# Two transformer layers on one core: the first two chains of each second MLP product issued together, and the first MLP rows normalised earlier

## Chip, core and metric

The kernel runs on one core of a Trainium2 chip. The metric is the device time of one execution in microseconds (us). TensorE (PE) multiplies; its sums lie in PSUM, 8 banks of 128 x 512 fp32. VectorE (DVE), ScalarE (ACT) and GpSimd (POOL) do the rest; SyncE (SP) issues nearly all DMAs. The engines run side by side, each works through its own list in order, and semaphores tie them together.

## The reference

An attention block and an MLP, both with a layer norm ahead and a residual, are applied twice with the same weights. 2048 rows of width 640, 32 heads of 20, hidden width 1536:

```python
x = x + _A_ref(_layernorm(x), wqkv, wo)            # softmax attention
x = x + _B_ref(_layernorm(x), w1, b1, w2, b2)
x = x + _A_ref(_layernorm(x), wqkv, wo)
x = x + _B_ref(_layernorm(x), w1, b1, w2, b2)

def _B_ref(x, w1, b1, w2, b2):
    h = einsum("bsd,df->bsf", x, w1) + b1
    r = where(h > 0, h, 0)
    return einsum("bsf,fd->bsd", r * r, w2) + b2
```

## The kernel before

Matrix operands are kept as two parts, hi (rounded) and lo (the rest), and a product is three matmuls: hi x hi, hi x lo, lo x hi (`THREE`, L323). A **chain** (L333) is the run of matmuls that sum into one PSUM bank; its first sets `start`, its last `stop`. `ps_all` (L95) hands out the 8 banks in turn, one for each chain, so a bank comes round again eight chains later.

`layer` (L1333) does one layer: the QKV projection, attention, and then, with all rows in four blocks of 512 (`qb`, each of four tiles `i` of 128 rows):

- **Output projection**, `add_heads` (L1240). For each of 4 row tiles and 2 halves of the width (`hf`), a chain of 15 matmuls (128x320), then a DVE add of the sum onto the row tile x (L1255), then `side()`. After both halves the tile is stored to `x_mid` in DRAM.
- **Transposing**, `transposed` (L1272), for the first MLP block only: the four normalised row tiles are turned by 20 PE transposes (L1277: five 128-column pieces k, four tiles i each), and each piece is split by ACT (hi, L256) and DVE (lo, L257) into `xnT`.
- **MLP**, `mlp` (L1285), four blocks, each in two halves of the hidden width (`fh`). The first product: for six tiles f of hidden units a chain of 15 matmuls (128x512); then ACT adds the bias and clips (r, L1300), DVE squares (L1301), ACT rounds to the hi part of h (L256), DVE forms its lo part (L257). The second product: for `hf` in 2 and `i` in 4 a chain of 18 matmuls (128x320), called y0 to y7 below, over the six h tiles in the order in which they were made, three matmuls each. So the last three matmuls of a chain read the newest h tile: two its hi part, one its lo part. A DVE add (L1320) takes the sum onto the row tile, then `side()`. In the first half POOL adds the bias b2 to the row tiles (L1307) after their loads; after y0 of the second half the next block's `xnT` is split from rows that were turned through DRAM (`parts`, L292, on ACT, DVE and POOL).

`side()` takes the next entry of a list `steps` and runs it: this is how work for what comes next gets between the chains. Ahead of the last output-projection block, `steps` gets ten entries that step the generator `normal_rows` (L1259) once each: the first issues the loads of rows 0 to 511 from `x_mid` on SP (L1261), four take the statistics of a tile (DVE L244 twice and L245, then two small POOL operations L247 and L248), four normalise a tile on DVE (L252), and the tenth ends it. The block has 8 chains, called C1 to C8 below, so eight entries run there; `all_steps()` behind it runs the other two. The order of each engine's work is that of the code; nothing reorders it.

After the projection SP has, in this order, the last of the `x_mid` stores, the loads of the rest of w1 and all of w2 (19 tiles of 480 to 512 KB), and the loads of the row tiles for the MLP.

## Time and profile before

| | us |
|---|---|
| median of 3 runs (lowest, highest) | 3569.83 (3569.45, 3570.3) |
| the profiled execution: its own time | 3570.51 |
| its span, first to last instruction | 3568.7 |

| stage, first layer | from about, us | to about, us |
|---|---|---|
| output projection, last block (C1 begins before the first add at 1434.96) | 1433 | 1450.0 |
| transposes of the first MLP rows | 1450.0 | 1453.8 |
| first MLP block, first product of the first half | 1453.8 | 1474.3 |
| its second product, y0 to y7 | 1474.3 | 1496.1 |
| second half: first product, second product | 1496.1 | 1538.3 |
| three more blocks | 1538.3 | 1797.6 |

The MLP of the second layer runs from 3226.8 to the end of the span. In the profile, an instruction's row gives the start, the duration, the engine, the line, output and inputs, how often it is merged, and in brackets how long its engine sat idle before it and who released it. Matmuls are pipelined: a 128x320 matmul is recorded with about 310 ns, while 127 of them in a row start at 1477.34 and the next ones at 1496.07, which is one each 147.5 ns.

### The profile page before, as it was taken

How to read it: one execution, taken by the hardware profiler on the slowest of the kernel's cores; microseconds unless marked ns; L12 is line 12 of the kernel's file. 1: busy time of each engine (PE TensorE's matmuls, PEld its weight loads, DVE VectorE, ACT ScalarE, POOL GpSimd, SP SyncE). 2: the span in 40 equal slices, each digit the busy share in tenths (PEclk: the TensorE clock that was granted, in tenths of full speed). 3: DMA queues.
4: the chain of work that ended last, by engine and by line, in shares of the span. 5: the costliest groups of instructions: out<-in, count | busy, mean ns of one | idle time of the engine just before them, and what ended most of it. 6: DMA issues, size and time to landing. Idle time of an engine off the chain costs nothing.

```text
span 3568.7 us, 70878 instructions
## 1 busy us (share of the span) xinstructions
PE 3551.0 (100%) x25544; PEld 2147.5 (60%) x25544; DVE 2636.6 (74%) x5088; ACT 2701.5 (76%) x4720; POOL 817.0 (23%) x929
## 2 busy tenths in 40 slices
PE   9999999999999999999999999999999999999999
PEld 7898333333333336889989973333333333378998
DVE  7998888888888881455569988888888888625443
ACT  5888999999999994122248889999999999932221
POOL 4430334321211210122153201212121212101110
PEclk9999999999999999999999999999999999999999
DMA  7666454422212136622367652232222121375221
GB/s 254 224 210 187 143 166 144 145 79 79 54 48 61 53 103 224 230 74 74 104 199 226 199 164 72 74 78 58 70 82 57 45 56 51 112 240 204 78 80 36
DMA packets 281598, 431.87 MB, mean 121 GB/s; under 512 B 70948, under 2 KB 130084, under 8 KB 281248
## 3 DMA queue, kind: packets, MB, share of 16 engines
q1 hardware_dynamic: 280720, 425.64, 38.6%
q8 instruction: 203, 3.33, 0.4%
q10 hardware_dynamic: 528, 1.70, 0.2%
q14 instruction: 147, 1.20, 0.1%
HBM read 282.52 MB, written 144.68 MB: 120 GB/s over the span
## 4 chain that ended last, share of the span: by engine, by line
PE 96%; ACT 1%; DMA 1%; DVE 1%; issue 0%; POOL 0%; SPq 0%; ACTq 0%; DVEq 0%; POOLq 0%
PE banks L771 28%; PE banks L336 22%; PE banks L756 18%; PE banks L662 17%; PE banks L356 6%; PE banks L368 5%; ACT e L766 1%; PE banks L351 1%; PE banks L469 0%; DMA kd<-d_kd 0%; DVE h L257 0%; DVE r L1301 0%; ACT r L1300 0%; ACT h L256 0%; SPq L76 0%
## 5 line engine op out<-in xcount | busy, mean ns | idle before, releaser
L766 ACT ACTIVATE e<-banks 128x512 f32<-128x512 f32 (+1 forms) x3416 | 2037.3, 690 | 49.3 <-PE banks L756 10.7
L673 DVE TENSOR_REDUCE mx<-banks 128x1 f32<-128x512 f32 x2560 | 1620.7, 685 | 322.6 <-PE banks L662 270.7
L771 PE MATMUL banks<-e,vg 128*32 128x512 f32 x8192 | 1093.4, 605 | 2.3 <-ACT e L766 2.3
L662 PE MATMUL banks<-k,q 60*128 60x512 f32 x3360 | 1060.4, 410 | 0.0
L756 PE MATMUL banks<-q,k 62*128 62x512 f32 x4096 | 1047.9, 441 | 0.7
L756 PEld LDWEIGHTS banks<-q,k 62*128 62x128 f32 x4096 | 515.4, 184 | 748.3 <-ACT e L766 493.5
L662 PEld LDWEIGHTS banks<-k,q 60*128 60x128 f32 x3360 | 566.3, 185 | 196.6 <-ACT e L766 65.6
L702 DVE CUSTOM_DVE_ANT_0 rl<-banks,rl 128x512 f32<-128x512 f32 x736 | 477.0, 689 | 36.2 <-PE banks L662 12.4
L695 ACT ACTIVATE rl<-banks 128x512 f32<-128x512 f32 x736 | 399.0, 601 | 58.1 <-PE banks L662 47.3
L771 PEld LDWEIGHTS banks<-e,vg 128*32 128x32 f32 x8192 | 162.2, 108 | 353.5 <-issue 271.1
L336 PE MATMUL banks<-w,h 128*128 128x320 f32 x2304 | 348.9, 310 | 2.7 <-DVE h L257 2.5
L1300 ACT ACTIVATE r<-banks,b_t 128x512 f32<-128x512 f32 x96 | 66.2, 689 | 375.6 <-PE banks L336 249.2
L336 PEld LDWEIGHTS banks<-w,h 128*128 128x128 f32 x2304 | 339.2, 188 | 11.4 <-DVE h L257 6.4
L336 PE MATMUL banks<-xnT,w 128*128 128x512 f32 x1440 | 329.7, 389 | 0.0
L368 PE MATMUL banks<-xnT,wqk 64*128 64x512 f32 x1080 | 326.5, 392 | 0.0
L356 PE MATMUL banks<-xnT,wqk 64*128 64x512 f32 x1080 | 326.2, 394 | 0.0
L336 PEld LDWEIGHTS banks<-xnT,w 128*128 128x128 f32 x1440 | 269.6, 188 | 55.3
L815 POOL TENSOR_TENSOR few<-few,minus_t 128x16 f32<-128x16 f32 x62 | 179.8, 2900 | 241.1 <-DMA few<-d_s 240.9
L662 PE MATMUL banks<-kd,q 60*128 60x512 f32 x736 | 211.3, 398 | 3.0 <-ACT rl L695 2.4
L368 PEld LDWEIGHTS banks<-xnT,wqk 64*128 64x128 f32 x1080 | 201.2, 187 | 9.2
L356 PEld LDWEIGHTS banks<-xnT,wqk 64*128 64x128 f32 x1080 | 199.0, 186 | 10.9 <-issue 1.7
L826 POOL TENSOR_TENSOR o<-o 128x512 f32<-128x512 f32 x62 | 79.5, 1283 | 519.1 <-DMA o<-d_r 280.5
(93 smaller groups left out, 2648.4 us busy)
## 6 DMA issues: line engine op xcount, KB each, us to landing
q<-d_qk SPq DMA_DIRECT2D x876, 80.0 KB
d_qk<-ev SPq DMA_DIRECT2D x80, 512.0 KB
k<-d_qk SPq DMA_DIRECT2D x444, 80.0 KB
x<-d_x SPq DMA_DIRECT2D x96, 320.0 KB
d_o<-ot SPq DMA_DIRECT2D x248, 80.0 KB
ot<-d_o SPq DMA_DIRECT2D x38, 512.0 KB
d_v<-v SPq DMA_DIRECT2D x32, 512.0 KB
vg<-d_v SPq DMA_DIRECT2D x32, 512.0 KB
```

The costliest lines, as they stand in the source:

```text
L336: nc.tensor.matmul(dst, a, b, start=(n == 0), stop=(n == last))
L356: top = nc.tensor.matmul(dst, a[:64], b[:64], start=start, stop=last)
L368: low = nc.tensor.matmul(dst, a, b, start=False, stop=last, skip_group_check=True)
L662: nc.tensor.matmul(dst, q_t[t][b : b + 60, p, sub * P : (sub + 1) * P], k_t[t // NQB, c][b : b + 60, p, :], start=True, stop=True,)
L673: nc.vector.tensor_reduce(maxima(t)[:, 2 * p + par, sub, c : c + 1], dst, axis=AX.X, op=ALU.max)
L695: nc.scalar.activation(r, dst, AF.Relu)
L702: nc.vector.tensor_tensor_reduce(out=r[par], in0=dst, in1=r[par], scale=1.0, scalar=LEAST, op0=ALU.add, op1=ALU.max, accum_out=maxima(t)[: ...
L756: nc.tensor.matmul(dst, k_t[t // NQB, kt // 4][b : b + 62, p, (kt % 4) * P : (kt % 4 + 1) * P], q_t[t][b : b + 62, p, :], start=True, stop ...
L766: nc.scalar.activation(dst, src, AF.Exp, scale=SCALE)
L771: nc.tensor.matmul(acc[32 * h : 32 * h + 32, :], v_t[t // NQB, kt // 8][:, kt % 8, 32 * h : 32 * h + 32], es[p][:, par, :], start=(kt == 0 ...
L815: nc.gpsimd.tensor_tensor(few, few, minus_t, op=ALU.pow)
L826: nc.gpsimd.tensor_mul(o[:, 0, :], o[:, 0, :], o[:, 1, :])
```

## The change

```diff
-    def chain(dst, pairs):
+    def chain(dst, pairs, part=None):
         last = len(pairs) - 1
-        for n, (a, b) in enumerate(pairs):
+        for n, (a, b) in list(enumerate(pairs))[part or slice(None)]:
             nc.tensor.matmul(dst, a, b, start=(n == 0), stop=(n == last))
...
             for hf in range(2):
                 c = slice(hf * HALF, (hf + 1) * HALF)
-                for i in range(4):
-                    dst = ps_all("y")
-                    chain(dst[:, :HALF], [
+                dsts = [ps_all("y") for _ in range(2)]
+
+                def down(i, part=None):
+                    chain(dsts[i][:, :HALF], [
                         (hs[f % 6][:, hx, i * P : (i + 1) * P], w_2.piece(at_2(f, hw, hf)))
                         for f in range(fh * 6, fh * 6 + 6)
                         for hx, hw in THREE
-                    ])
-                    x = xs[i]
+                    ], part)
+
+                for i in range(4):
+                    if i > 1:
+                        dsts.append(ps_all("y"))
+                    if hf or i > 1:
+                        down(i)
+                    elif i == 0:
+                        for part in (slice(15), slice(15, 18)):
+                            for j in range(2):
+                                down(j, part)
+                    x, dst = xs[i], dsts[i]
                     nc.vector.tensor_add(x[:, c], dst[:, :HALF], x[:, c])
...
                 norm = normal_rows(0, x_m, rows)
-                steps.extend([lambda: next(norm, None)] * 10)
+                steps.extend([lambda: (next(norm, None), next(norm, None))] * 5)
             add_heads(qb, x_a, x_m, xs, side)
```

Of each second product (16 in all: 2 layers, 4 blocks, 2 halves) the chains y0 and y1 are now issued as four pieces: 15 matmuls of y0, 15 of y1, the last 3 of y0, the last 3 of y1. Matmuls, banks and their turn are as before. The generator that loads and normalises the first MLP rows is stepped twice behind each of C1 to C5, in place of once behind each of C1 to C8 and twice behind the block.

PE in the first MLP block, second product: h_16523 is the fifth h tile, h_16547 the newest, w_... are tiles of w2; the rows stand at the end of y0 and at the end of y1.

```order
@@ -6226,5 +6226,4 @@
 L336 MATMUL banks<-w_16386,h_16523 128x320
 L336 MATMUL banks<-w_16384,h_16523 128x320
-L336 MATMUL banks<-w_16386,h_16547 128x320 x3
 L336 MATMUL banks<-w_16380,h_16430 128x320 x3
 L336 MATMUL banks<-w_16380,h_16451 128x320
@@ -6236,5 +6235,5 @@
 L336 MATMUL banks<-w_16386,h_16523 128x320
 L336 MATMUL banks<-w_16384,h_16523 128x320
-L336 MATMUL banks<-w_16386,h_16547 128x320 x3
+L336 MATMUL banks<-w_16386,h_16547 128x320 x6
 L336 MATMUL banks<-w_16380,h_16430 128x320 x3
 L336 MATMUL banks<-w_16380,h_16451 128x320
```

The newest tile is first read as the 16th matmul of the product before, as the 31st now, behind the 15 of y1.

DVE in the last block of the first layer's output projection: x_16019 is the block's first row tile, x_16054 its second, x_16183 to x_16189 are the four MLP row tiles. First the place where their statistics begin, before:

```order
L1255 TENSOR_TENSOR x_16019<-banks,x_16019 128x320 x2
L244 BN_STATS bst_16207<-x_16183 128x6 x2
L245 BN_AGGR mv_16208<-bst_16207 128x2
L1255 TENSOR_TENSOR x_16054<-banks,x_16054 128x320
L244 BN_STATS bst_16231<-x_16185 128x6 x2
L245 BN_AGGR mv_16232<-bst_16231 128x2
```

and now:

```order
L1255 TENSOR_TENSOR x_16019<-banks,x_16019 128x320
L244 BN_STATS bst_16191<-x_16183 128x6 x2
L245 BN_AGGR mv_16192<-bst_16191 128x2
L1255 TENSOR_TENSOR x_16019<-banks,x_16019 128x320
L244 BN_STATS bst_16214<-x_16185 128x6 x2
L245 BN_AGGR mv_16215<-bst_16214 128x2
L244 BN_STATS bst_16221<-x_16187 128x6 x2
L245 BN_AGGR mv_16222<-bst_16221 128x2
L1255 TENSOR_TENSOR x_16054<-banks,x_16054 128x320
```

The first statistics stand ahead of the add of C2 instead of behind it. Then, on the same engine, the end of the block (x_16089 and x_16124 are its last two row tiles, the last row is the first split for the MLP), before:

```order
L1255 TENSOR_TENSOR x_16089<-banks,x_16089 128x320
L252 TENSOR_SCALAR x_16183<-x_16183,mv_16208 128x640
L1255 TENSOR_TENSOR x_16124<-banks,x_16124 128x320
L252 TENSOR_SCALAR x_16185<-x_16185,mv_16232 128x640
L1255 TENSOR_TENSOR x_16124<-banks,x_16124 128x320
L252 TENSOR_SCALAR x_16187<-x_16187,mv_16255 128x640
L252 TENSOR_SCALAR x_16189<-x_16189,mv_16279 128x640
L257 TENSOR_TENSOR xnT_16349<-banks,xnT_16349 128x512
```

and now:

```order
L252 TENSOR_SCALAR x_16183<-x_16183,mv_16192 128x640
L1255 TENSOR_TENSOR x_16054<-banks,x_16054 128x320
L252 TENSOR_SCALAR x_16185<-x_16185,mv_16215 128x640
L252 TENSOR_SCALAR x_16187<-x_16187,mv_16222 128x640
L1255 TENSOR_TENSOR x_16089<-banks,x_16089 128x320
L252 TENSOR_SCALAR x_16189<-x_16189,mv_16246 128x640
L1255 TENSOR_TENSOR x_16089<-banks,x_16089 128x320
L1255 TENSOR_TENSOR x_16124<-banks,x_16124 128x320 x2
L257 TENSOR_TENSOR xnT_16349<-banks,xnT_16349 128x512
```

The last two normalisations stood behind the add of C8; now the last one stands behind the add of C5 and ahead of those of C6 to C8. On SP, ACT and POOL the order of the instructions is the same before and after.

## The prediction

> **What bounds the kernel now.** The page says first that PE is busy throughout, at the full granted clock in all 40 slices:

> ```profile
> span 3568.7 us, 70878 instructions
> PE 3551.0 (100%) x25544; PEld 2147.5 (60%) x25544; DVE 2636.6 (74%) x5088; ACT 2701.5 (76%) x4720; POOL 817.0 (23%) x929
> PEclk9999999999999999999999999999999999999999
> ```

> The change removes no matmul, so it can give back only time in which PE stands still or starts late. I therefore read next the list of PE's own waits:

> ```profile
> PE banks L336 <- DVE h L257: 2.5, 15, 0.2
> PE banks L1277 <- DVE x L252: 2.2, 4, 0.9
> ```

> These are the two waits that the two edits aim at: matmuls of the second product that wait for the lo part of the newest h, in 15 of 16 products, and transposes that wait for a normalised row. Together 4.7 us of idle time. But idle time is measured from the recorded end of the matmul before, and a recorded matmul (0.31 us) is more than twice as long as the distance at which matmuls follow one another. So I count by starts, in the timeline of PE around one block:

> ```profile
> 1474.30 2.88 PE L336 MATMUL banks<-w,h 128*128 128x320 f32 x17
> 1477.34 18.89 PE L336 MATMUL banks<-w,h 128*128 128x320 f32 x127 [0.17 <-DVE h L257]
> 1496.07 20.59 PE L336 MATMUL banks<-xnT,w 128*128 128x512 f32 x90
> 1516.50 2.94 PE L336 MATMUL banks<-w,h 128*128 128x320 f32 x17
> 1519.61 18.89 PE L336 MATMUL banks<-w,h 128*128 128x320 f32 x127 [0.17 <-DVE h L257]
> ```

> From 1477.34 to 1496.07 there are 127 matmuls, one each (1496.07 - 1477.34) / 127 = 0.1475 us. The 17 ahead of the wait should take 17 x 0.1475 = 2.51 us. They take 1477.34 - 1474.30 = 3.04 us in the first half and 1519.61 - 1516.50 = 3.11 us in the second. **So PE loses 0.53 us and 0.60 us there**, not 0.17. The second layer shows the same (3.05 and 3.10 us in its first and last half):

> ```profile
> 3247.32 2.88 PE L336 MATMUL banks<-w,h 128*128 128x320 f32 x17
> 3250.37 0.85 PE L336 MATMUL banks<-w,h 128*128 128x320 f32 x4 [0.17 <-DVE h L257]
> ...
> 3542.91 2.94 PE L336 MATMUL banks<-w,h 128*128 128x320 f32 x17
> 3546.01 0.56 PE L336 MATMUL banks<-w,h 128*128 128x320 f32 x2 [0.17 <-DVE h L257]
> ```

> [...]

> **First edit: the order of y0 and y1.** The timeline at the end of y0 shows when the parts of the newest h are there:

> ```profile
> 1475.94 0.62 ACT L256 CAST h<-r 128x512 fp32r<-128x512 f32 x1 [0.76 <-DVE r L1301]
> 1476.60 0.69 DVE L257 TENSOR_TENSOR h<-r,h 128x512 fp32r<-128x512 f32 x1 [0.69 <-ACT h L256]
> 1476.61 0.30 PEld L336 LDWEIGHTS banks<-w,h 128*128 128x128 f32 x2 [0.23 <-ACT h L256]
> ```

> The hi part is there at 1476.56 (PE's weight load waited for it), the lo part at 1477.29, by work of ACT and DVE that the edit doesn't touch. Now 30 matmuls stand ahead of the newest tile: hi is needed at 1474.30 + 30 x 0.1475 = 1478.73 and lo, the 33rd matmul, at 1474.30 + 32 x 0.1475 = 1479.02. The margins are 2.2 and 1.7 us, so the wait goes whole. In the second half everything is 0.07 us later; the margin stays over 1.6 us. Gain: 8 first halves x 0.53 + 7 second halves x 0.60 = 4.24 + 4.20 = **8.4 us**. (The sixteenth product, in the first layer's last block, has transposes of the next layer between the last first-product chain and y0, and had no wait.)

> What is late next? y0 ends at its 33rd matmul rather than its 18th: its add comes 1479.02 - 1477.34 = 1.7 us later than before, y1's add 0.4 us earlier (36th matmul at 1474.30 + 35 x 0.1475 = 1479.46, against 1477.34 + 18 x 0.1475 = 1480.0). Behind y0's add DVE has side work and, in the second half, eight small subtractions for the next block. No row after it is needed by PE soon: the bank comes round only after eight chains, and in the first block the adds already run far behind without PE waiting, because they wait for POOL's bias add:

> ```profile
> 1480.76 0.49 DVE L1320 TENSOR_TENSOR x<-banks,x 128x320 f32<-128x320 f32 x1 [3.47 <-POOL x L1307]
> ```

> y0's bank is first wanted again by the chain that begins at 1496.07, now 2 us earlier, 13 us behind that add. This cover, seven chains of 2.65 us, would have to be gone before the edit cost anything. Cost taken: 0.

> One thing has no row: PE returning to a sum that it left open in another bank. Each pair has 3 changes of bank where it had 1, so 32 more in all. A plain change of bank shows nothing: the 127 matmuls hold seven, at 0.1475 us, and attention returns to its open bank 7 about a thousand times (8192 recorded matmuls in groups of 8) with 2.3 us of PE idle before them:

> ```profile
> L771 PE MATMUL banks<-e,vg 128*32 128x512 f32 x8192 | 1093.4, 605 | 2.3 <-ACT e L766 2.3
> ```

> That column can hide 0.31 - 0.1475 = 0.16 us at each, as shown above; so the bounds are 0 and 32 x 0.16 = 5.1 us. A gain is excluded, since no matmul gets shorter. I take 0, the end that both rows are nearest to.

> **Second edit: rows normalised two steps at a time.** DVE in the last projection block of the first layer, and PE behind it:

> ```profile
> 1442.19 0.89 DVE L244 BATCH_NORM_STATS2 bst<-x 128x6 f32<-128x320 f32 x2 [4.54 <-DMA x<-d_x]
> 1443.12 0.21 DVE L245 BATCH_NORM_AGGREGATE mv<-bst 128x2 f32<-128x12 f32 x1
> 1443.24 0.48 DVE L1255 TENSOR_TENSOR x<-banks,x 128x320 f32<-128x320 f32 x1
> 1443.63 0.88 DVE L244 BATCH_NORM_STATS2 bst<-x 128x6 f32<-128x320 f32 x2
> ...
> 1447.82 0.61 DVE L252 TENSOR_SCALAR x<-x,mv 128x640 f32<-128x640 f32 x1
> 1448.35 0.48 DVE L1255 TENSOR_TENSOR x<-banks,x 128x320 f32<-128x320 f32 x1
> ...
> 1450.36 0.49 DVE L1255 TENSOR_TENSOR x<-banks,x 128x320 f32<-128x320 f32 x1 [1.01 <-PE banks L336]
> 1450.77 1.12 DVE L252 TENSOR_SCALAR x<-x,mv 128x640 f32<-128x640 f32 x2
> ```

> ```profile
> 1450.16 0.38 PE L1277 MATMUL banks<-ident,x 128*128 128x128 f32 x2
> 1451.42 0.33 PE L1277 MATMUL banks<-ident,x 128*128 128x128 f32 x1 [0.88 <-DVE x L252]
> 1451.95 2.07 PE L1277 MATMUL banks<-ident,x 128*128 128x128 f32 x17 [0.20 <-DVE x L252]
> 1453.78 20.68 PE L336 MATMUL banks<-xnT,w 128*128 128x512 f32 x90
> ```

> The transposes follow at (1453.78 - 1451.95) / 17 = 0.108 us; all 20 from 1450.16 would end at 1452.31 and not 1453.78. **At stake: 1.47 us in each layer.** Will the rows be ready? The loads are issued behind C1 as before, so the statistics still begin at 1442.19. By starts, statistics of a tile take 1.05 us, an add 0.39, a normalisation 0.53. Ahead of the end of the last normalisation stand now 4 x 1.05 + 4 x 0.39 + 3 x 0.53 + 0.61 = 7.96 us: 1450.15. The third tile's row, the nearest case, is ready at 1442.19 + 4.2 + 3 x 0.39 + 3 x 0.53 = 1449.2. The fourth transpose would start at 1450.16 + 3 x 0.108 = 1450.48. All are ready: the wait goes whole, 1.47 us. Then come the adds of C6 to C8, 3 x 0.39, until 1451.3; the first split on DVE follows the fourth transpose by 1452.98 - 1451.95 = 1.03 us, so at 1451.51. Still in time, with 0.2 us to spare.

> In the second layer the rows come later against PE:

> ```profile
> 3215.68 0.89 DVE L244 BATCH_NORM_STATS2 bst<-x 128x6 f32<-128x320 f32 x2 [5.02 <-DMA x<-d_x]
> ...
> 3223.16 0.38 PE L1277 MATMUL banks<-ident,x 128*128 128x128 f32 x2
> ```

> The last row is ready at 3215.68 + 7.96 = 3223.64, the fourth transpose could start at 3223.48: about 0.2 us of wait stays, and 1.3 us of 1.47 is gained. Together **2.7 us**; the bounds are 0 (DVE as late as now) and 2.9.

> The added wait: DVE's first statistics, with its 4.5 us for the load, now stands ahead of the add of C2. Behind it wait that add, C2's bank (wanted eight chains later, by the second transposed piece at about 1450.6, the add then being done by 1443.6) and the store of the first row tile, for which nobody waits on PE's side. The last store follows the add of C8, which ends at 1451.3 rather than 1450.36 + 0.49 = 1450.85 (in the second layer about 1 us later), and SP's 19 weight loads follow that store, so they start up to 1 us later. At the rate of the next row a tile of 0.51 MB takes 1.25 us; w2's first four tiles, behind three of w1, land 7 x 1.25 = 9 us after about 1452, well before their use at 1474.30 - 1.47 = 1472.8:

> ```profile
> 1460.00:1465.00 5.00, 5.00 (x23) 4.13 (x22) 1.71 (x3) 2.00 (x3) 0.00 (x0) 1.00 1.02 409
> ```

> (The last number is GB/s, the one ahead of it the DMA share.) Cost taken: 0.

> **The sum.** 8.4 + 2.7 = 11.1 us. The profiled execution took 3570.51 (span 3568.7 and 1.8 around it), 0.68 above the median of the runs: it would take 3559.4, and the median 3569.83 becomes 3558.7.

> **The rivals.**
> 1. *Returning to an open sum costs PE something*, up to the bound of 5.1 us: gain 6.0 to 11, say 8.5, 3561.3. For it: no row isolates it. Against: attention's row. Chance 0.08.
> 2. *The idle column is the true loss*: 2.5 + 2.2 = 4.7 us, 3565.1. Against: the count by starts above. Chance 0.06.
> 3. *The rows come no earlier*, because loads land later or DVE's longer queue at C6 to C8 holds the first split: only the first edit, 8.4 us, 3561.4. For it: the spare time is 0.2 us in one layer and none in the other. Chance 0.08.
> 4. *DVE's adds bind PE.* y0 and y1 end 0.44 us apart, so y0's add of 0.49 us lies beside 3 matmuls of y1 rather than 18. If PE waited for it each time, 16 x 0.49 = 7.8 us would be given back: 3566.5. Against: eight banks, and the adds at 1480.76. Chance 0.02. [...]
> 5. *Slower: switching banks in the middle of a sum drains PE.* Place: the 32 added changes. It turns the sign from 11.1 / 32 = 0.35 us each, over twice the bound; at 0.5 us it would be 4.9 us slower, 3574.7. Chance 0.03.
> 6. *It doesn't do what it says*: no change, 3569.8. Against: PE's order shows all six reads of the newest tile behind both chains. Chance 0.01.

> **How the numbers follow.** The forecast has 0.72: 3558.7. Its low end is 11.3 us of gain plus the scatter of the runs (0.4) and as much again for knock-on shifts in the second attention: about 3557.3. The high end takes in rival 1 to its bound and rival 3: 3569.83 - 6.0 = 3563.8. That holds 0.72 + 0.08 + 0.08 = 0.88; leaving out rivals 2 and 4 to 6. A measurement of this kernel can tell about 0.2% (7.1 us) from no change, so faster means below 3562.7. Forecast, rival 3 and three quarters of rival 1 give 0.86 for faster; the rest of rival 1, and rivals 2, 4 and 6, 0.11 for the same; rival 5, 0.03 for slower.

> **What would show it.** In PE's waits, the line for DVE h falls from 15 times to none or one, and the 36 matmuls of a pair start 36 x 0.1475 = 5.31 us before the next chain; if they take 5.8, rival 1. The first transposes take 2.2 us from first to the start of the MLP, not 3.6; if a wait for DVE x of about 1 us stays, rival 3. The time from the first y matmul to the next first product falls from 21.77 to about 21.24 us; if it falls by 0.17 only, rival 2. New waits of PE for DVE L1331 (the add's line now) would mean rival 4. The prediction is wrong if attention, which the change doesn't touch, differs by more than 1 us.

## The result, and the profile after

The changed kernel took 3557.5 us (5 runs, 3556.65 to 3557.91), beside it the kernel before 3570.3 us (5 runs): 12.8 us less, a ratio of 0.9963 with a 95% interval of 0.9952 to 0.9975. The prediction started from 3569.83; 0.9963 of that is 3556.6, and 12.8 us off it is 3557.0; both lie below the low end of the range (3557.3). The direction came as forecast, one wait went whole and the other nearly; the gain was larger than the 11.1 us of the sum and than the range allowed.

The page of the changed kernel and the list of PE's waits, answering to the first lines of the prediction:

```profile
span 3555.2 us, 70874 instructions
PE 3542.0 (100%) x25544; PEld 2145.5 (60%) x25544; DVE 2630.3 (74%) x5088; ACT 2701.5 (76%) x4720; POOL 818.6 (23%) x929
PEclk9999999999999999999999999999999999999999
```

```profile
PE banks L662 <- ACT rl L695: 2.5, 6, 0.8
PE banks L771 <- ACT e L766: 2.3, 6, 0.7
PE banks L486 <- POOL ident masks.py:199: 1.4, 1, 1.4
PE banks L498 <- DVE x L252: 1.3, 2, 0.7
PE banks L469 <- DVE x L252: 0.7, 1, 0.7
PE banks L1277 <- DVE x L252: 0.2, 1, 0.2
```

The wait for h is gone from all 15 products. Of the wait for normalised rows 0.2 us is left. No other line has grown by more than 0.4 us. Yet the span is 13.5 us shorter, and the two lines lost only 4.5 us of idle time. Where the rest lies shows in PE's timeline of the first block, by starts:

```profile
1449.56 2.46 PE L1277 MATMUL banks<-ident,x 128*128 128x128 f32 x20
1451.78 20.70 PE L336 MATMUL banks<-xnT,w 128*128 128x512 f32 x90
1472.31 21.28 PE L336 MATMUL banks<-w,h 128*128 128x320 f32 x144
1493.42 20.59 PE L336 MATMUL banks<-xnT,w 128*128 128x512 f32 x90
```

The 144 matmuls of a second product now run as one piece, 1493.42 - 1472.31 = 21.11 us, so 0.1466 us each. Before they took 21.77 us (1474.30 to 1496.07), and 21.84 in second halves (1516.50 to 1538.34). That is 0.66 and 0.73 us for a product, not 0.53 and 0.60. The transposes up to the MLP take 1451.78 - 1449.56 = 2.22 us instead of 3.62; in the second layer a wait remains:

```profile
3216.32 0.49 PE L1277 MATMUL banks<-ident,x 128*128 128x128 f32 x3
3216.98 2.08 PE L1277 MATMUL banks<-ident,x 128*128 128x128 f32 x17 [0.17 <-DVE x L252]
3218.81 0.95 PE L336 MATMUL banks<-xnT,w 128*128 128x512 f32 x3
```

3218.81 - 3216.32 = 2.49 us instead of 3.62. The sum from the profile is 8 x 0.66 + 7 x 0.73 + 1.40 + 1.13 = 5.28 + 5.11 + 2.53 = 12.9 us, against 12.8 by the medians. The remaining 0.6 us between the two spans lies ahead of the first output projection, in code that the change doesn't touch; over the profiles that point lies anywhere between 1377.92 (two between, below) and 1378.80 us (the kernel before), so it is scatter.

### The profile page after: what moved, and what is told of

The parts are those of the page before. It is cut to its first block, busy times and chain, and to the rows that moved or that the text cites. A ratio compares the mean times of both kernels' runs of the same rounds, so it can differ in the third digit from the quotient of the medians.

```text
span 3555.2 us, 70874 instructions
## 1 busy us (share of the span) xinstructions
PE 3542.0 (100%) x25544; PEld 2145.5 (60%) x25544; DVE 2630.3 (74%) x5088; ACT 2701.5 (76%) x4720; POOL 818.6 (23%) x929
## 4 chain that ended last, share of the span: by engine, by line
PE 96%; DMA 1%; ACT 1%; DVE 1%; POOL 1%; issue 0%; SPq 0%; POOLq 0%; ACTq 0%; DVEq 0%
PE banks L771 28%; PE banks L336 22%; PE banks L662 18%; PE banks L756 17%; PE banks L356 5%; PE banks L368 5%; PE banks L351 1%; ACT e L766 1%; SPq L76 0%; DMA x<-d_x 0%; PE banks L469 0%; DMA few<-d_s 0%; DVE bst L244 0%; DMA q<-d_qk 0%; DMA x<-in_A_x_dram 0%
## 5 line engine op out<-in xcount | busy, mean ns | idle before, releaser
L766 ACT ACTIVATE e<-banks 128x512 f32<-128x512 f32 (+1 forms) x3416 | 2037.3, 691 | 49.2 <-PE banks L756 10.7
L771 PE MATMUL banks<-e,vg 128*32 128x512 f32 x8192 | 1093.4, 605 | 2.3 <-ACT e L766 2.3
L771 PEld LDWEIGHTS banks<-e,vg 128*32 128x32 f32 x8192 | 162.1, 108 | 352.2 <-issue 268.0
L336 PE MATMUL banks<-w,h 128*128 128x320 f32 x2304 | 341.2, 309 | 0.0
L336 PEld LDWEIGHTS banks<-w,h 128*128 128x128 f32 x2304 | 339.1, 188 | 1.2
L336 PE MATMUL banks<-xnT,w 128*128 128x512 f32 x1440 | 329.7, 389 | 0.0
L336 PEld LDWEIGHTS banks<-xnT,w 128*128 128x128 f32 x1440 | 269.5, 188 | 55.3
L268 POOL CAST mr<-nt 128x32 fp32r<-128x32 f32 x64 | 13.4, 210 | 807.0 <-DVE nt L728 807.0
```

Of the source, the lines that this page charges most:

```text
L336: nc.tensor.matmul(dst, a, b, start=(n == 0), stop=(n == last))
L766: nc.scalar.activation(dst, src, AF.Exp, scale=SCALE)
L771: nc.tensor.matmul(acc[32 * h : 32 * h + 32, :], v_t[t // NQB, kt // 8][:, kt % 8, 32 * h : 32 * h + 32], es[p][:, par, :], start=(kt == 0 ...
```

## The experiments

Beside every kernel, the kernel before ran on the same chip; times are medians, gains are against that neighbour. A product is one of the 15 second products that waited before, measured from its first matmul to the first one of the next chain. Theory A: a wait costs PE its delay and about 0.10 us more behind each release. Theory B: the prediction's 0.53 and 0.60 us are the whole price, and the missing 1.7 us came from elsewhere.

### One edit at a time

The first edit alone (the second's line put back):

```diff
-                steps.extend([lambda: (next(norm, None), next(norm, None))] * 5)
+                steps.extend([lambda: next(norm, None)] * 10)
```

> The first edit alone: y0 and y1 in four pieces, rows normalised one step per chain as before. Theory A (a wait in the stream costs PE its delay and, on top, about 0.10 us after each release, because the released matmul is followed after 0.25 us and not after 0.147): a pair is worth 21.77 - 21.11 = 0.66 us in first halves and 0.73 in second halves, so 8 x 0.66 + 7 x 0.73 = 10.4 us faster than before, and each second product takes 21.11 us from its first matmul to the next first product. Theory B (the prediction's 0.53 and 0.60 are the whole price of the wait, and the rest of the 12.8 us came from elsewhere): 8.4 us faster.

Measured: 3559.13 us against 3569.59, 10.5 us faster (ratio 0.997, 0.9957 to 0.9982). Every product takes 21.12 us. Theory A has the size; the missing time is in the products themselves.

The second edit alone:

```diff
-                steps.extend([lambda: next(norm, None)] * 10)
+                steps.extend([lambda: (next(norm, None), next(norm, None))] * 5)
```

> The second edit alone. Both theories: transposes and their wait take 2.22 us in the first layer and 2.49 in the second, where they took 3.62 in both: 1.4 + 1.1 = 2.5 us faster than before. If the missing 2 us belong to this edit (later stores, other DMA traffic), 4 to 5 us faster. The second products keep 21.77 and 21.84 us.

Measured: 3568.61 us against 3569.59, 1.0 us faster (0.9997, 0.9988 to 1.0005: not told apart from nothing by time alone). Its profile has 2.10 us in the first layer, 1.5 us gained as expected, but 3.31 us in the second, 0.3 us gained. DVE's rows there, in the profile of the second edit alone, show why:

```profile
3214.08 0.89 DVE L244 BATCH_NORM_STATS2 bst<-x 128x6 f32<-128x320 f32 x2 [7.53 <-DMA x<-d_x]
3215.01 0.21 DVE L245 BATCH_NORM_AGGREGATE mv<-bst 128x2 f32<-128x12 f32 x1
3215.13 0.44 DVE L1255 TENSOR_TENSOR x<-banks,x 128x320 f32<-128x320 f32 x1
3216.28 0.89 DVE L244 BATCH_NORM_STATS2 bst<-x 128x6 f32<-128x320 f32 x2 [0.71 <-DMA x<-d_x]
```

The second row tile was not there when DVE wanted it: 0.71 us of wait that the prediction had not counted. In the profile of the kernel before, the second row was wanted as soon (1.44 us behind the start of the first statistics) and was there; here its statistics begin 2.20 us behind the first. So it landed later against the first row, and no row shows why.

### How late may the newest h come?

These three kernels change only how many matmuls of y1 stand ahead of the last three of y0 (15 in the changed kernel): 2, 4 or 5.

```diff
-                        for part in (slice(15), slice(15, 18)):
-                            for j in range(2):
-                                down(j, part)
+                        for j, part in ((0, slice(15)), (1, slice(2)), (0, slice(15, 18)), (1, slice(2, 18))):
+                            down(j, part)
```

> The changed kernel, but with only 2 matmuls of y1 ahead of the last three of y0, then the other 16 of y1. The hi part is then wanted at 17 x 0.1466 = 2.49 us behind the first matmul (ready at 2.26), the lo part at 19 x 0.1466 = 2.79 (PE was released at 3.04 in first halves, 3.11 in second halves). One wait of 0.25 and 0.32 us comes back. Theory A adds 0.10 us each: 8 x 0.35 + 7 x 0.42 = 5.7 us slower than the changed kernel, so about 7 us faster than before. Theory B: 8 x 0.25 + 7 x 0.32 = 4.2 us slower than the changed kernel, 8.5 us faster than before.

Measured: 3564.1 us against 3569.59, 5.5 us faster where theory A said about 7. Products take 21.49 us in first and 21.54 in second halves: a loss of 0.38 and 0.43 us each, where theory A said 0.35 and 0.42 and theory B 0.25 and 0.32. Over 15 products 6.0 us; another 0.8 us goes in the second layer's transposes (3.25 us here, 2.49 in the changed kernel). PE's timeline of this kernel is the most telling of the study:

```profile
1471.91 21.65 PE L336 MATMUL banks<-w,h 128*128 128x320 f32 x144
1493.40 20.59 PE L336 MATMUL banks<-xnT,w 128*128 128x512 f32 x90
1513.83 2.94 PE L336 MATMUL banks<-w,h 128*128 128x320 f32 x19
1516.93 18.59 PE L336 MATMUL banks<-w,h 128*128 128x320 f32 x125 [0.17 <-DVE h L257]
1535.37 0.86 PE L336 MATMUL banks<-xnT,w 128*128 128x512 f32 x3
```

In the first half PE loses 0.38 us and the profile shows no idle time at all: the delay fits into the record of the matmul before. In the second half it shows 0.17 and loses 0.43.

> The changed kernel with 4 matmuls of y1 ahead of the last three of y0. The lo part is wanted at 21 x 0.1466 = 3.08 us behind the first matmul: in first halves (release at 3.04) no wait, 21.11 us for a product. In second halves (3.11) 0.03 us of wait. Theory A with a price for each release however short the wait: 0.13 us in 7 second halves, 0.9 us slower than the changed kernel. Theory B: 0.2 us slower.

Measured: 3560.23 us against 3570.37. Products take 21.19 and 21.25 us, 0.08 and 0.14 us lost:

```profile
1472.07 21.35 PE L336 MATMUL banks<-w,h 128*128 128x320 f32 x144
1493.26 20.59 PE L336 MATMUL banks<-xnT,w 128*128 128x512 f32 x90
1513.69 21.41 PE L336 MATMUL banks<-w,h 128*128 128x320 f32 x144
1534.94 20.59 PE L336 MATMUL banks<-xnT,w 128*128 128x512 f32 x90
```

Second halves are as theory A said; first halves, where the lo part is there 0.04 us ahead of its matmul's turn, were to lose nothing and lose 0.08. So the limit isn't the matmul's turn but a point ahead of it.

> The changed kernel with 5 matmuls of y1 ahead of the last three of y0. Four between left 0.08 us in first halves (the lo part there 0.04 us ahead of its matmul's turn) and 0.13 in second halves (0.03 behind it). Theory A, corrected: what has to be in time is the weight load, about 0.11 us ahead of the matmul's turn. With five between, the turn is at 22 x 0.1466 = 3.23 us, the load's at 3.12, and h at 3.04 or 3.11: no loss, 21.11 us for every product, the same span within 0.2 us from the MLP's start to the next projection as in the changed kernel. If each product that touches h late pays a fixed 0.1 us for another reason, 21.19 to 21.24 us remain.

Measured: 3557.39 us (one run), every product 21.11 us. That is as the corrected theory forecast. The turn is at 3.23 us, so the lo part is released 0.19 us ahead of it in first halves and 0.12 in second ones, and nothing is lost; with four between it was 0.04 ahead and 0.03 behind, and 0.08 and 0.14 were lost. In these two kernels the loss is what the release lacks of 0.11 us ahead of the turn, to 0.01 us.

### Only the lo part in time

```diff
-                        for part in (slice(15), slice(15, 18)):
+                        for part in (slice(17), slice(17, 18)):
```

> The changed kernel with the cut behind the 17th matmul instead of the 15th: 17 of y0, 17 of y1, the last one of y0, the last one of y1. The lo part is in time, the hi part is wanted at 15 x 0.1466 = 2.20 us behind the first matmul and there at 2.26, PE's matmul for it started at 2.32 in first halves of the kernel before (0.07 later in second halves). Theory A: 0.13 us of delay and 0.10 after the release, so 21.34 us in first halves and 21.41 in second halves; 8 x 0.23 + 7 x 0.30 = 4.0 us slower than the changed kernel. Theory B: 8 x 0.13 + 7 x 0.20 = 2.4 us slower.

Measured: 3562.21 us against 3570.37. Products take 21.34 us in first halves and 21.40 to 21.41 in second ones: theory A to the hundredth, 3.9 us over 15 products. The time agrees: 3.8 us more than the changed kernel beside it (3558.43, below).

### Does returning to an open sum cost anything?

```diff
-                    if hf or i > 1:
+                    if i > 1:
                         down(i)
                     elif i == 0:
-                        for part in (slice(15), slice(15, 18)):
+                        cuts = [(n, n + 1) for n in range(18)] if hf else [(0, 15), (15, 18)]
+                        for lo, hi in cuts:
                             for j in range(2):
-                                down(j, part)
+                                down(j, slice(lo, hi))
```

> The changed kernel, and in the second half of the width (where nothing is waited for) y4 and y5 alternate matmul by matmul: 35 changes of bank where there was 1, so 16 x 34 = 544 more returns to an open sum. Theory A: a return costs nothing, same time as the changed kernel within 0.5 us. Rival 1 of the prediction (a return costs up to 0.16 us): up to 87 us slower; every 1 us would be 1.8 ns for one return. If pairing by itself makes matmuls cheaper (a way to explain the missing 2 us without the wait): about 2 us faster than the changed kernel.

Measured: 3559.48 us against 3569.59. Products take 21.11 and 21.12 us, as in the changed kernel, with 34 more returns in each: at 0.01 us for 34 a return costs under 0.3 ns. Rival 1 is out, and pairing doesn't make matmuls cheaper. The kernel still gained only 10.1 us; some is lost in the second layer's first transposes (3.46 us), and some in the first layer's last block, where the next layer's rows are normalised behind the adds:

```profile
1783.74 0.38 PE L469 MATMUL banks<-ident,x 128*128 128x128 f32 x2
1784.86 0.33 PE L469 MATMUL banks<-ident,x 128*128 128x128 f32 x1 [0.73 <-DVE x L252]
1785.38 1.20 PE L469 MATMUL banks<-ident,x 128*128 128x128 f32 x9 [0.20 <-DVE x L252]
1786.34 2.89 PE L336 MATMUL banks<-w,h 128*128 128x320 f32 x18
```

From the first of these transposes to the next chain it takes 1786.34 - 1783.74 = 2.60 us; in the changed kernel 1.23. y4's add comes only when both chains are nearly done, the normalisations behind it on DVE are late, and there PE does wait. The same edit that is free where PE needs nothing from behind the add costs 1.4 us where it does.

### The cover of the adds

```diff
+    ps_y = Ring(6, 7)
...
-                dsts = [ps_all("y") for _ in range(2)]
+                dsts = [ps_y("y") for _ in range(2)]
...
-                        dsts.append(ps_all("y"))
+                        dsts.append(ps_y("y"))
```

> The changed kernel with the cover of the adds taken away: the chains of the second product get banks 6 and 7 in turn instead of all eight, so y2 has to wait for y0's add. Rival 4 of the prediction names 16 x 0.49 = 7.8 us for such a wait. By rows: y0's last matmul starts 32 x 0.1466 = 4.69 us behind the first, its add starts 0.45 later and takes 0.49, so y2 could start at 5.7 where it is due at 5.28: 0.4 us, and 0.1 after the release, in 16 products: 8 us; in second halves eight subtractions (3.7 us) stand ahead of y1's add and y3 waits about 1.5 us more, 8 x 1.5 = 12 us; in each layer's first block the adds run some 3 us late: 6 us or more. In all 20 to 35 us slower than the changed kernel. If it costs under 3 us, the eight banks are no cover that mattered.

Measured: 3586.81 us against 3570.49, 16.3 us slower than before, while the changed kernel was 11.9 and 12.8 us faster than before: a difference of about 28 us. The first product of each layer takes 26.1 and 26.6 us, the others 21.6 to 22.6. Part of this is the clock, which fell to half for 3.41 us in each layer (last section): the 108 matmuls behind the wait took 1498.56 - 1481.09 = 17.47 us there, and 3283.41 - 3265.94 = 17.47, against 1669.71 - 1653.78 = 15.93 in a product without the dip, about 1.5 us each. PE's waits of MLP chains for an add (this kernel's lines count one more):

```profile
PE banks L337 <- DVE x L1332: 12.2, 13, 3.7
```

As elsewhere in this study, the idle column shows less than the time lost. So the reason for taking rival 4 at nothing was the right one: with eight banks the late adds stay off PE, with two they don't.

### Where the row loads stand

```diff
             if qb + 1 == NQB:
-                rows = []
-                norm = normal_rows(0, x_m, rows)
                 steps.extend([lambda: (next(norm, None), next(norm, None))] * 5)
             add_heads(qb, x_a, x_m, xs, side)
+            if qb + 2 == NQB:
+                rows = []
+                norm = normal_rows(0, x_m, rows)
+                next(norm)
             for s in range(qb * 4, min(qb * 4 + 4, w_1.n)):
                 w_1.load(s)
```

The changed kernel ran beside it:

> The changed kernel once more, as the neighbour of the three runs beside it. Both theories: 12.0 to 13 us faster than before (10.4 from the pairs, 1.4 to 1.5 from the first layer's rows, 0.2 to 1.1 from the second layer's, where the rows land between 6.7 and 7.5 us ahead of the first transpose). Not under 11.5.

> The changed kernel, but the four loads of the first MLP rows are issued one projection block earlier in the list, ahead of the four loads of w1 tiles instead of behind them. If what is left of the second layer's wait (0.17 us idle in the changed kernel's profile, 0.6 to 0.8 in the runs before this) is the landing of these rows behind 2 MB of weights, it goes: 2.10 us from the first transpose to the MLP in both layers, 0.5 to 1.5 us faster than the changed kernel. If DVE's queue holds the rows, nothing changes in the profile, same time.

Measured: the changed kernel 3558.43 us (3557.73 to 3561.16), with the rows' loads first 3556.63 us (3556.22 to 3557.17), against 3570.37 before: 11.9 and 13.7 us faster (0.9967, 0.9955 to 0.998; 0.9961, 0.9949 to 0.9974). The first is just under the 12.0 expected, the second more than expected. The runs of the two don't overlap. In the profile with the loads first DVE begins its statistics 12.6 us ahead of the first transpose and the transposes don't wait:

```profile
3203.31 0.89 DVE L244 BATCH_NORM_STATS2 bst<-x 128x6 f32<-128x320 f32 x2 [2.10 <-DMA x<-d_x]
```

```profile
3215.92 2.34 PE L1277 MATMUL banks<-ident,x 128*128 128x128 f32 x20
3218.02 1.18 PE L336 MATMUL banks<-xnT,w 128*128 128x512 f32 x4
```

2.10 us in both layers. The statistics also stand one step earlier in DVE's list here, since the loads no longer take the first step. But in the changed kernel DVE's place in the list held nothing up; DVE stood idle for the loads:

```profile
3208.87 0.89 DVE L244 BATCH_NORM_STATS2 bst<-x 128x6 f32<-128x320 f32 x2 [7.26 <-DMA x<-d_x]
```

So what was left of that wait was the landing of the rows behind the w1 tiles, not DVE's queue: from the first row load's issue to the statistics it takes 3203.31 - 3199.40 = 3.9 us here, and 3208.87 - 3202.01 = 6.9 us in the changed kernel. By its gain, this is the fastest version of the study.

The other way, later:

```diff
-                steps.extend([lambda: (next(norm, None), next(norm, None))] * 5)
+                steps.extend([None] * 3 + [lambda: (next(norm, None), next(norm, None))] * 5)
```

> The changed kernel with the row loads and all steps three chains later, behind C4 to C8. The loads are then issued 6.6 us later, and all four rows are normalised some 5 us behind the end of the projection: PE stands nearly still for 4 to 6 us in each layer. If a landing that leaves PE sparse for about 3 us makes the clock fall (as in one profile of the changed kernel, 0.5 for about 3 us at 3220 to 3223), the granted clock now falls in both layers and each loses 1.5 us or more beyond its wait: 10 to 16 us slower than the changed kernel in all. If that dip had another cause, the clock stays at 1.00 and the loss is the wait alone, 8 to 12 us.

Measured: 3559.92 us against 3570.49, 10.6 us faster: 1.3 to 2.2 us less than the changed kernel gained, where 8 to 16 were expected. The expectation took an instruction's place in the code for its time. SP in this kernel:

```profile
1433.91 1.86 SPq L76 DMA_DIRECT2D w<-d_w  x4
1437.89 0.32 SPq L76 DMA_DIRECT2D d_x<-x  x1
1438.26 2.18 SPq L76 DMA_DIRECT2D x<-d_x  x4
```

Written behind C4, the loads wait on SP for nothing but the store of the first row tile, behind C2's add, and go out at 1438.26, 2.65 us later than before and not 6.6. The statistics begin at 1443.64, the last row is ready at 1451.58 where the fourth transpose was due at 1450.69, and the transposes take 3.09 us. In the second layer the first transpose is 0.3 us late and they take 4.20 us. The clock stayed at 1.00 in this profile; what that says comes in the last section.

## Why the prediction was too low

**The size of the first edit: 8.4 us forecast, 10.4 in the profile and 10.5 measured alone.** The step that failed is "The 17 ahead of the wait should take 17 x 0.1475 = 2.51 us". The pitch was averaged over the 127 matmuls that begin with the one released by the wait. Undisturbed it is 21.11 / 144 = 0.1466 (so the 147.5 ns given ahead of the prediction is too long as well). The difference looks like nothing, but over 127 matmuls it is 0.11 us, and that was part of the loss, booked as pitch (over the 17 it is 0.02 more: 0.53 + 0.11 + 0.02 = 0.66). The rows around the release in the kernel before show it:

```profile
1477.34 0.59 PEld L336 LDWEIGHTS banks<-w,h 128*128 128x128 f32 x4 [0.43 <-DVE h L257]
1477.34 0.71 PE L336 MATMUL banks<-w,h 128*128 128x320 f32 x3 [0.17 <-DVE h L257]
```

Elsewhere a weight load starts ahead of its matmul: 0.14 us in a running chain, just behind the start of the matmul before (1475.61 and 1475.76), and 0.23 us at the start of the product (1474.07 and 1474.30). Here h is the weight operand, so the load waits as well and both start at 1477.34; the released matmul is recorded with 0.41 us instead of 0.31, and the next one follows it after 0.25.

That the loss of this lead is the 0.11 us which the prediction missed is a reading of these rows; no run took the lead away by itself.

The starts of the weight loads in the trace of the kernel before, taken to the nanosecond, bear the reading out. In a running chain a load starts 0.003 us behind the matmul before its own (1475.611 and 1475.614). A load that waits for h starts later, and the next load follows it after 0.11 us (1477.341 and 1477.449). The loss is then (lag of the waiting load behind the matmul before) + 0.107 - 0.147. Lags of 0.270 us (hi) and 0.475 (lo) give 0.23 and 0.43, together the 0.66 measured; in the second half 0.333 and 0.475 give 0.29 and 0.43, where 0.73 was measured. With two between, the row of the second half above has the released matmul 1516.93 - 1513.83 = 3.10 us behind the first, so 0.46 us behind the one before it (18 x 0.1466 = 2.64, an estimate): that gives 0.42, where 0.43 was measured.

Counted by turns, one rule fits the measured losses of the kernels in the table to 0.02 us: the loss is (release + 0.11) - (the matmul's turn), if that is positive. Release is counted from the product's first matmul, 2.32 us for hi and 3.04 for lo in first halves (in second halves 0.07 more). The 0.11 was read from the kernel before and from four between; five between was forecast with it:

| matmuls between | turn of | loss by the rule, first / second half | measured |
|---|---|---|---|
| 0 (before) | hi 2.20, then lo 2.72 / 2.79 | 0.23 + 0.43 = 0.66 / 0.30 + 0.43 = 0.73 | 0.66 / 0.73 |
| 17 / 1 cut | hi 2.20 | 0.23 / 0.30 | 0.23 / 0.30 |
| 2 | lo 2.79 | 0.36 / 0.43 | 0.38 / 0.43 |
| 4 | lo 3.08 | 0.07 / 0.14 | 0.08 / 0.14 |
| 5 | lo 3.23 | 0 / 0 | 0 / 0 |
| 15 (changed) | lo 4.69 | 0 / 0 | 0 / 0 |

**The margins and what is late next were right.** The wait went in all 15 products; y0's later add bound nothing, and the two-bank run showed that the eight banks are the reason.

**The second edit: 2.7 us forecast, 2.5 in the profile of the changed kernel, less in most others.** The first layer gave its 1.40 to 1.52. In the second layer the step that all rows are there from 1.05 us to 1.05 us on, because the first one is, nearly held in two profiles: that of the changed kernel (1.13 us gained) and that with five between, where the transposes take 3219.22 - 3216.83 = 2.39 us (1.23 gained):

```profile
3216.83 2.63 PE L1277 MATMUL banks<-ident,x 128*128 128x128 f32 x20
3219.22 20.68 PE L336 MATMUL banks<-xnT,w 128*128 128x512 f32 x90
```

In six other profiles with this edit as it stands, and with the clock at 1.00 there, these transposes took 3.05 to 3.46 us, a gain of 0.2 to 0.6: the first row came later against PE, or the second one later against the first. Rival 3, the loads landing late, is half true in that layer.

**The sum** was 11.1 us; with the first edit at its true size the same working gives 13.1, and the change measured 12.8 and 11.9. The 11.9 would lie inside the range (3569.83 - 11.9 = 3557.9), but its profile shows products of 21.11 us as well, so what fell short there is the second edit; a hit of that kind would be luck and doesn't mend the first term. The low end of the range stands for 12.5 us of gain, while the terms named for it (11.3 and twice 0.4) add up to 12.1; they hold scatter and shifts, and no bound for the pitch, which was a term of the sum as well.

**Rivals.** 1: out (alternating). 2: out; the idle lines lost 4.5 us, the time 12.8. 3: as above. 4: its mechanism is real with two banks, absent with eight. 5 and 6: no.

Not settled: why, with the second edit and the loads behind the w1 tiles, the first row's statistics begin 7.4 us ahead of the second layer's transposes in two profiles and 5.5 to 7.3 us in others, and why the second row is sometimes late as well; the traces show only when they did.

## What to carry to other kernels

Price a wait of PE by starts against the pitch of a stretch that holds no wait, never by the idle column: 0.17 us of idle was 0.43, and 0.38 could show none. What PE needs as weights had to be ready 0.11 us ahead of its matmul's turn here, so put enough independent matmuls ahead of it (five would do, fifteen were given). When a wait for a computed row is removed, look at once at the load behind it: moving four loads ahead of four larger ones was worth 1.8 us more against the changed kernel beside it (0.9 against its first measurement), where the edit alone had given 1.0.

## What the hardware showed beyond that

In one profile of the changed kernel the granted clock fell. There the rows landed late (9.5 us of wait ahead of the first statistics), and PE started four transposes in 2.4 us (3217.14 to 3219.50). The windows of that profile (start and end in us, length, then the time and count of PE, PEld, DVE, ACT and POOL, the granted clock, the DMA share, GB/s):

```profile
3216.81:3220.22 3.41, 1.89 (x12) 1.14 (x11) 3.41 (x9) 0.31 (x1) 1.15 (x2) 1.00 0.25 96
3220.22:3223.64 3.42, 3.42 (x16) 3.23 (x15) 3.11 (x7) 2.53 (x5) 0.00 (x0) 0.50 0.88 289
3223.64:3227.05 3.41, 3.41 (x16) 2.80 (x16) 0.49 (x1) 0.36 (x1) 0.00 (x0) 1.00 0.92 359
```

The clock was at half for 3.41 us, after PE had become sparse and not while it was. The last 17 transposes and the first product behind them took 3222.39 - 3219.50 = 2.89 and 3243.49 - 3222.39 = 21.10 us, against 1.83 and 3239.33 - 3218.81 = 20.52 in the other profile of the changed kernel: 1.6 us more. That execution took 3561.16 us, 2.7 more than the median of its kernel. The kernel with two banks shows the same in each layer, behind an add wait of 3.23 and one of 3.73 us:

```profile
1478.38:1481.79 3.41, 0.70 (x5) 0.70 (x6) 0.49 (x1) 0.00 (x0) 2.81 (x2) 1.00 1.04 395
1481.79:1485.20 3.41, 3.41 (x15) 3.41 (x14) 2.45 (x7) 0.00 (x0) 3.41 (x4) 0.50 0.40 151
3263.55:3266.96 3.41, 1.02 (x7) 1.02 (x8) 0.55 (x2) 0.00 (x0) 3.13 (x3) 1.00 1.04 396
3266.96:3270.37 3.41, 3.41 (x15) 3.41 (x15) 2.39 (x7) 0.00 (x0) 3.33 (x4) 0.50 0.21 81
```

```profile
3217.92:3221.33 3.41, 2.03 (x14) 1.52 (x14) 2.33 (x6) 0.83 (x2) 0.71 (x1) 1.00 0.30 96
```

How little PE must do for the clock to fall was not measured: at the end of the kernel before, the step from 3562.89 to 3566.30 with 2.01 us of recorded PE time was followed by a step at 1.00, where the one with 1.89 us, with sparse transposes in it, was followed by the dip above. The dip may not be confined to these two profiles. Four other kernels with the second edit (two between, four between, only the lo part in time, late rows) have five executions whose mean granted clock is 0.999, as in the profile with the dip; they are the slowest of their kernels, 1.7 to 3.6 us above the medians. No execution of the kernel before, or of the second edit alone, has it. The version with the loads first has no such stretch, and all its five runs lie within 1 us.
